# The eighth w1 row of each partition by five small loads of its own, and fewer small VectorE operations, in a one-core decode kernel

## The chip, the cores and the metric

The kernel runs on one core of one Trainium2 chip. The metric is device time in microseconds (us) of one execution; lower is better. Engines are named as in the profile: PE is TensorE's matmul, PEld its weight load, DVE is VectorE, ACT is ScalarE, POOL is GpSimd, SP is SyncE, whose queue issues nearly all loads here.

## What is computed

One token of a decoder: grouped-query attention over a key/value cache, and a small MLP block beside it, both on the same normalized input, summed with the input.

```python
x  = A_x; xn = layernorm(x)                      # 1 x 1024
out = x + A(xn, k_cache, v_cache, wq, wo) + B(xn, w1, w2, w3, w4)
# A: 32 query heads, 4 key/value heads, 65536 keys of 128
q = (xn @ wq);  p = softmax(q k^T / sqrt(128));  A = (p v) @ wo
# B: h = gelu(layernorm(xn) @ w1), quarters of h shifted by one or two tokens
x1 = xn + shifted(h) @ w2
B  = x1 + gelu(layernorm(x1) @ w3) @ w4          # w3: 1024 x 3584, w4: 3584 x 1024
```

With one token, each shift of the quarters brings in nothing but zeros, so h @ w2 adds zero; the kernel computes it all the same. All matrices and the cache are bfloat16: 169.87 MB are read from HBM once.

## The kernel before

The work is a list of items: wq, then for each key/value head g and each half r of its keys a K block and a V block (8.39 MB each), with w3, "wa" (w1 and the first half of w4), "wb" (the rest of w4, and w2) and wo between them. Three SBUF slots of 64 KB a partition take the items in turn. `load(i)` (L211) issues item i's DMAs on SP's queue once the readers of that slot are done; the main loop (L566) computes item i and then issues the load of item i + 3. In the order of the list: wq, K(0,0), V(0,0), w3, K(0,1), V(0,1), wa, K(1,0), V(1,0), K(1,1), and so on; wb stands before the last V, wo at the end, in five pieces (`WO_PIECES`).

Weights lie with one row block a partition: of w1 (1024 x 1024) partition p holds rows 8p to 8p + 7, so each partition reads 16 KB in one piece, and `rows_product` (L314) multiplies column c of the normalized input with row c of every partition, c from 0 to 7, in two chunks of 512 columns that lie in different column groups of TensorE (`tile_position`).

K blocks are transposed 32 by 32 on VectorE (L449, four of 4.4 us), multiplied with the queries (L455, 64 matmuls), reduced to a maximum (L462), turned into exponentials on ScalarE (L471), and transposed again (L473). V blocks are multiplied by these (L503). At the end of a head `group_weights` (L479) and `group_end` (L513) scale and fold the halves; the last lines (L524 to L529) put a head's result into oT as bfloat16. `compute_wa` (L405) multiplies by w1 (L408), applies gelu (L410), moves the row into columns (L419 to L425) and adds the first half of w4's product (L426, L337).

Order is kept by a small recorder, `Flow`: each operation names keys that it reads and writes, and waits on semaphores for the last writer and the readers of these. An engine's own order is the order in the code. A load's semaphore counts 16 when it is complete. The setup (L243 to L286) builds identity matrices on GpSimd and masks from them on VectorE, while the first loads are on their way.

Of the kernel before, what the change touches and what calls it, by code (L numbers as in the profile page):

```python
# [16 lines left out]
WO_PIECES = (10, 10, 8, 3, 1)  # L17
WO_UNROLL = 5
CGS = 2


class Flow:
# [75 lines left out]
def kernel(  # L98
# [43 lines left out]
    def tile_sb(shape, dtype, name):  # L142
        return sb.tile(shape, dtype, name=name)
# [27 lines left out]
    hf_f = tile_sb([P, FC], F32, "hf_f")  # L171
    hT = tile_sb([P, FC], BF16, "hT")
    gT = tile_sb([P, DC], BF16, "gT")
    o5 = tile_sb([P, 32], F32, "o5")
    oT = tile_sb([P, OC], BF16, "oT")
    rep = msk[0:1].rearrange("p a b -> p (a b)")

    sc = ps.tile([P, HF, 512], F32, name="sc")
# [6 lines left out]
    w3_v = B_w3.rearrange("(p c) f -> p (c f)", c=DC)  # L185
    w4_v = B_w4.rearrange("(m c) n -> m (c n)", c=FC)
    wo_v = A_wo.rearrange("(m c) n -> m (c n)", c=OC)
    w1_v = B_w1.rearrange("(p c) n -> p (c n)", c=DC)
    w2_v = B_w2.rearrange("(m c) n -> m (c n)", c=DC)
    assert sum(WO_PIECES) == OC  # L190
    wo_start = [sum(WO_PIECES[:i]) for i in range(len(WO_PIECES))]
# [19 lines left out]
    def load(i):  # L211
        item, s = items[i], slot_of[i]
        t, kind = slots[s], items[i][0]
        if kind == "wq":
            loads = [(0, wq_v)]
        elif kind == "w3":
            loads = [(0, w3_v)]
        elif kind == "wa":
            loads = [(0, w1_v), (KEYS // 2, w4_v[:, 0:FH * NOUT])]
        elif kind == "wb":  # L220
            loads = [(0, w4_v[:, FH * NOUT:FC * NOUT]), (KEYS // 2, w2_v)]
        elif kind == "wo":
            loads = [(wo_start[q] * NOUT, wo_v[:, wo_start[q] * NOUT:(wo_start[q] + n) * NOUT])
                     for q, n in enumerate(WO_PIECES)]
        else:
            cache = A_k_cache if kind == "K" else A_v_cache
            _, g, r = item
            loads = [(0, cache[0, g, r * KEYS:(r + 1) * KEYS, :].rearrange("(p k) d -> p (k d)", p=P))]
        fl._wait("Q", [], [("slot", s), ("slot", s, 1)] + [("slot", s, q) for q in range(2, 5)] + [("kt", s, cg) for cg in range(4)])
        for n, (at, src) in enumerate(loads):  # L230
            key = ("slot", s) if n == 0 else ("slot", s, n)
            fl.dma("Q", f"slot{s}" if n == 0 else f"slot{s}_{n}", [], [key], t[:, at:at + src.shape[-1]], src)

    qrow = work[:, 0:1024].rearrange("p (b n) -> p b n", b=2)
    psel = work[:, 1024:1536].rearrange("p (b m) -> p b m", b=4)
# [26 lines left out]
    def v(reads, writes, call):  # L262
        one("V", reads, writes, call)

    v(["ident_f"], ["sel32"], lambda e: e.tensor_tensor(out=sel32[:], in0=ident_f[:, 0:32], in1=ident_f[:, 32:64], op=ALU.add))
    v(["ident_f", "sel32"], ["sel32"], lambda e: e.tensor_tensor(out=sel32[:], in0=sel32[:], in1=ident_f[:, 64:96], op=ALU.add))
    v(["ident_f", "sel32"], ["sel32"], lambda e: e.tensor_tensor(out=sel32[:], in0=sel32[:], in1=ident_f[:, 96:128], op=ALU.add))
# [5 lines left out]
    v(["sel8"], ["sel8x"], lambda e: e.tensor_copy(out=sel8x[:].rearrange("p (h dd) -> p h dd", dd=4),  # L273
                                                   in_=sel8[:].unsqueeze(2).to_broadcast([P, 8, 4])))
    iv = ident_bf[:].rearrange("p (b i r) -> p b r i", b=2, r=2)
    for b in range(2):
        for par in range(2):
            v(["ident_bf"], [("psel", b, par)], lambda e: e.tensor_copy(
                out=psel[:, 2 * b + par, :].rearrange("p (a i) -> p a i", a=4),
                in_=iv[:, b, par, :].unsqueeze(1).to_broadcast([P, 4, 32])))  # L280
    psel_keys = [("psel", b, par) for b in range(2) for par in range(2)]
    lead = ident_bf[:].rearrange("p (j u) -> p j u", u=32)[:, :, 0]
    v(["ident_bf", "hstrip"], ["hstrip"], lambda e: e.tensor_copy(
        out=hstrip[:, 64:128].rearrange("p (j m) -> p j m", j=4), in_=lead.unsqueeze(2).to_broadcast([P, 4, 16])))
    v(["ident_bf"], ["gsel"], lambda e: e.tensor_copy(
        out=gsel[:].rearrange("p (j m) -> p j m", j=2), in_=lead[:, 0:2].unsqueeze(2).to_broadcast([P, 2, 64])))  # L286

    def layernorm(src, src_key, n):
# [22 lines left out]
    v([("rs", 0)], ["ln_s1"], lambda e: e.tensor_scalar(out=ln_s1, in0=rs1, scalar1=1.0, scalar2=None, op0=ALU.add))  # L311
    v([("neg", 0), ("rs", 0)], ["ln_s2"], lambda e: e.tensor_tensor(out=ln_s2, in0=neg1, in1=rs1, op=ALU.mult))

    def rows_product(s, keys, wt, width, n_chunks):  # L314
        def emit(signal):
            for c in range(DC):
                for j in range(4):
                    for bk in range(2):
                        ch = 4 * bk + j
                        if ch < n_chunks:  # L320
                            ins = nc.tensor.matmul(sc[32 * j:32 * j + 32, bk, 0:width], lhsT=xpad[:, c, :],  # L321
                                                   rhs=wt[:, c, ch * width:(ch + 1) * width],
                                                   start=(c == 0), stop=(c == DC - 1), tile_position=(0, 32 * j),
                                                   skip_group_check=True)
            signal(ins)
        op("T", keys + ["xpad"], ["sc"], emit)

# [15 lines left out]
    def fill_qst(g, eng):  # L343
        for a in range(4):
            sl = slice(32 * a, 32 * a + 32)
            one(eng, ["qsel"], [("qst", g % 2)],
                lambda e: e.tensor_copy(out=qst[g % 2][sl, :, 24 + 32 * a:24 + 32 * a + 8], in_=qsel[sl, :, 8 * g:8 * g + 8]))  # L347

    def compute_wq(s):
# [20 lines left out]
            signal(ins)  # L370
        op("T", ["qT"] + psel_keys, ["pm"], emit2)
        v(["pm"], ["qsel"], lambda e: e.tensor_copy(out=qsel[:], in_=pq))
        fill_qst(0, "V")
        fill_qst(1, "G")
        v(["xn2b", "xpad"], ["xpad"], lambda e: e.tensor_copy(out=xpad[:, :, 0:1], in_=xn2b[:].unsqueeze(2)))
        v(["xr", "ln_s1", "ln_s2"], ["ob"], lambda e: e.tensor_scalar(
# [9 lines left out]
    def compute_w3(s):  # L386
        wt = slots[s][:, 0:DC * F].rearrange("p (c n) -> p c n", n=F)
        rows_product(s, [("slot", s)], wt, FW, 8)
        hrow = work[:, 0:2 * FW].rearrange("p (b n) -> p b n", b=2)
        one("S", ["sc"], ["hrow", "work"], lambda e: e.activation(out=hrow, in_=sc[:, 0:2, 0:FW], func=ACTF.Gelu_apprx_tanh))  # L390

        def emit(signal):
            for bk in range(2):
                ins = nc.tensor.matmul(pm[:, 0:FW], lhsT=hstrip[:, 64 - 64 * bk:192 - 64 * bk], rhs=hrow[:, bk, :],  # L394
                                       start=(bk == 0), stop=(bk == 1))
            signal(ins)
        op("T", ["hrow", "hstrip"], ["pm"], emit)
        hm = work[:, 1024:1024 + 2 * FW].bitcast(F32).rearrange("p (a c) -> p a c", c=FC)
        v(["pm", "mask16"], ["hm"], lambda e: e.tensor_tensor(  # L399
            out=hm, in0=pm[:, 0:FW].rearrange("p (a c) -> p a c", c=FC),  # L400
            in1=mask16[:].unsqueeze(2).to_broadcast([P, 16, FC]), op=ALU.mult))
        v(["hm"], ["hf_f"], lambda e: e.reduce_sum(out=hf_f[:], in_=hm.rearrange("p a c -> p c a"), axis=AX.X))
        v(["hf_f"], ["hT"], lambda e: e.tensor_copy(out=hT[:], in_=hf_f[:]))

    def compute_wa(s):  # L405
        slot = slots[s]
        wt = slot[:, 0:DC * D].rearrange("p (c n) -> p c n", n=D)
# [5 lines left out]
        for grp, shift in enumerate((1, -1, 2, -2)):  # L413
# [10 lines left out]
        v(["gm"], ["gf"], lambda e: e.reduce_sum(out=lnb[:, 7], in_=gm.rearrange("p a c -> p c a"), axis=AX.X))  # L424
        v(["gf"], ["gT"], lambda e: e.tensor_copy(out=gT[:], in_=lnb[:, 7]))  # L425
# [53 lines left out]
    def group_weights():  # L479
# [33 lines left out]
    def group_end(g):  # L513
# [4 lines left out]
        if g == HKV - 1:  # L518
# [8 lines left out]
        v(["msk"], ["o5"], lambda e: e.tensor_reduce(out=o5[rows, :], in_=msk[rows].rearrange("p dd c -> p c dd"),  # L527
                                                     axis=AX.X, op=ALU.add))
        v(["o5"], ["oT"], lambda e: e.tensor_copy(out=oT[rows, :], in_=o5[rows, :]))  # L529

    fold = work[0:1, :].bitcast(F32)
    started = [False] * 4
# [73 lines left out]
```

## Time and profile before

| what | us |
|---|---|
| median of three runs (402.16 to 402.35) | 402.19 |
| the profiled execution | 402.23 |
| its span in the profile | 400.1 |
| PE busy | 223.5 (56%) |
| DVE busy | 210.5 (53%) |
| ACT busy | 30.9 (8%) |
| POOL busy | 6.3 (2%) |
| SP's main DMA queue (q1), share of 16 engines | 98.3% |
| DMA, mean over the span | 425 GB/s |

The profile is of one execution; what lies between its span and its own time, 2.1 us, is start and end of the execution. A line of a view by time gives the start, the busy time, the engine, the line of the code and the operation; in brackets, how long the engine sat idle before and what released it. A line of the queues gives the queue, its kind, packets, MB and its share of the 16 DMA engines in the window asked for; a packet counts in the window in which it starts, so shares of short windows can be above 100%. A line by stretch gives the window, its length, the busy time of each engine with its instructions, the granted TensorE clock, the DMA share and GB/s. The trace also has each DMA packet's start, duration and size, and the time of each of the completions (one per DMA engine that took part) by which a load counts its semaphore up.

### The profile page before, as it was taken

Reading aid. Unit: us, or ns where it says so; the run is one execution under the profiler, and the core shown is the slowest. Engines: PE = TensorE matmul, PEld = TensorE weight load, DVE = VectorE, ACT = ScalarE, POOL = GpSimd, SP = SyncE. Lnnn points to the kernel's source line nnn. Section 1 sums busy time; section 2 is a strip of 40 time slices with the busy share of each in tenths; the row PEclk is TensorE's granted clock in tenths of the full one; section 3 lists DMA queues with packets and bytes.
Section 4 is the critical chain, followed back from the end, with each engine's and each line's share of the span. In section 5 each row is a group of like instructions: output and inputs, shape, how many; then the busy total and the mean of one; then the engine's idle time right before and its main releaser. Section 6 shows DMA issues by size and latency. Waiting matters only on the chain.

```text
span 400.1 us, 4118 instructions
## 1 busy us (share of the span) xinstructions
PE 223.5 (56%) x1407; PEld 91.3 (23%) x1407; DVE 210.5 (53%) x191; ACT 30.9 (8%) x36; POOL 6.3 (2%) x28
## 2 busy tenths in 40 slices
PE   0263087360195563964395608845925194596985
PEld 0220033130042220421142203312402041232332
DVE  2201792210962448822972499269455963794421
ACT  1000000320001300003001000020020002000200
POOL 3000000000000000000000000000000000000000
PEclk9995579585589598795699567968988599799799
DMA  8999999999989999999999999999999999999995
GB/s 347 465 446 419 420 414 454 391 473 452 426 382 471 451 426 414 426 432 432 465 434 426 419 426 439 426 472 428 426 419 434 439 419 459 398 454 434 397 432 208
DMA packets 4054, 170.02 MB, mean 425 GB/s; under 512 B 582, under 2 KB 588, under 8 KB 844
## 3 DMA queue, kind: packets, MB, share of 16 engines
q1 hardware_dynamic: 3896, 169.87, 98.3%
q8 instruction: 8, 0.13, 0.1%
q10 hardware_dynamic: 148, 0.00, 0.0%
q14 instruction: 2, 0.02, 0.0%
HBM read 169.87 MB, written 0.00 MB: 425 GB/s over the span
## 4 chain that ended last, share of the span: by engine, by line
DMA 53%; PE 28%; DVE 13%; issue 4%; ACT 1%; SPq 1%; POOL 0%; ACTq 0%
DMA slot<-in_A_k_cache_dram 46%; PE sc L455 20%; DVE slot L449 10%; DMA slot<-in_A_wo_dram 7%; PE oacc L503 5%; PE psR L337 2%; DVE sm L462 2%; DVE work L473 1%; ACT work L471 1%; SPq L89 1%; PE sc L321 0%; DVE og L515 0%; ACT L471 0%; DVE sm L464 0%; PE pm L463 0%
## 5 line engine op out<-in xcount | busy, mean ns | idle before, releaser
L455 PE MATMUL sc<-slot,qst 128*128 x512 | 127.8, 407 | 77.4 <-DVE slot L449 76.4
L449 DVE STREAM_TRANSPOSE slot<-slot 128x4096 f32<-128x4096 f32 x32 | 139.4, 4413 | 29.7 <-DMA slot<-in_A_k_cache_dram 29.7
L455 PEld LDWEIGHTS sc<-slot,qst 128*128 128x128 bf16 x512 | 51.8, 101 | 154.2 <-issue 106.8
L503 PE MATMUL oacc<-slot,work 128*32 128x512 bf16 x512 | 45.7, 530 | 37.5 <-DVE work L473 21.9
L462 DVE TENSOR_REDUCE sm<-sc 128x1 f32<-128x2048 f32 x8 | 18.3, 2291 | 58.4 <-PE sc L455 58.4
L503 PEld LDWEIGHTS oacc<-slot,work 128*32 128x32 bf16 x512 | 19.0, 127 | 60.8 <-issue 56.9
L473 DVE STREAM_TRANSPOSE work<-work 128x2048 bf16<-128x2048 bf16 x8 | 18.5, 2312 | 21.2 <-ACT work L471 21.2
L471 ACT ACTIVATE work<-sc,sm 128x2048 bf16<-128x2048 f32 x8 | 15.7, 1967 | 147.1 <-DVE sm L469 147.1
L337 PE MATMUL psR<-slot,hT 128*1 x56 | 16.2, 438 | 0.5 <-issue 0.2
L515 DVE SCALAR_TENSOR_TENSOR og<-oacc,sm,og 128x128 f32<-128x128 f32 x16 | 5.6, 351 | 18.6 <-PE oacc L503 18.2
L321 PE MATMUL sc<-slot,xpad 128*32 128x512 bf16 (+1 forms) x144 | 11.1, 441 | 4.3 <-DMA slot<-in_A_wq_dram 4.3
L471 ACT ACT_TABLE_LOAD x3 | 3.8, 1283 | 117.5 <-DVE sm L469 117.5
L463 PE MATMUL pm<-ident_f,sm 128*1 128x128 f32 x8 | 2.2, 270 | 19.1 <-DVE sm L462 19.1
L294 PE MATMUL pm<-sm,og 128*128 128x1 f32 x4 | 1.2, 363 | 14.9 <-DVE sm L293 14.9
L337 PEld LDWEIGHTS psR<-slot,hT 128*1 x56 | 5.1, 92 | 10.9 <-issue 7.8
L321 PEld LDWEIGHTS sc<-slot,xpad 128*32 128x32 bf16 x144 | 5.4, 113 | 9.0 <-DMA slot<-in_A_wq_dram 4.4
L399 DVE TENSOR_TENSOR work<-pm,mask 128x448 f32<-128x448 f32 x1 | 0.6, 624 | 11.0 <-PE pm L394 11.0
L463 PEld LDWEIGHTS pm<-ident_f,sm 128*1 128x1 f32 x8 | 0.6, 79 | 23.0 <-DVE sm L462 23.0
L352 DVE CAST work<-sc 128x512 bf16<-128x512 f32 x1 | 0.7, 690 | 9.2 <-PE sc L321 9.2
L347 POOL COPY qst<-qsel 32x32 bf16<-32x32 bf16 x12 | 2.5, 206 | 189.0 <-PE sc L455 161.8
L337 PE MATMUL psR<-slot,oT 128*1 x20 | 4.5, 379 | 1.6 <-DVE oT L529 1.6
L509 ACT COPY ob<-oacc 128x512 f32<-128x512 f32 x4 | 2.3, 585 | 33.1 <-PE oacc L503 33.1
(99 smaller groups left out, 71.6 us busy)
## 6 DMA issues: line engine op xcount, KB each, us to landing
slot<-in_B_w_dram SPq DMA_DIRECT2D x1, 7168.0 KB, 50.8
slot<-in_B_w_dram SPq DMA_DIRECT2D x2, 3584.0 KB, 31.9
slot<-in_A_wo_dram SPq DMA_DIRECT2D x2, 2560.0 KB, 19.5
slot<-in_B_w_dram SPq DMA_DIRECT2D x2, 2048.0 KB, 30.1
slot<-in_A_wo_dram SPq DMA_DIRECT2D x1, 2048.0 KB, 26.7
slot<-in_A_wo_dram SPq DMA_DIRECT2D x1, 768.0 KB, 28.1
slot<-in_A_wo_dram SPq DMA_DIRECT2D x1, 256.0 KB, 28.4
slot<-in_A_k_cache_dram SPq DMA_DIRECT2D x8, 36.1
```

The lines of the kernel that those rows point to most:

```text
L89: self.engines[eng].dma_start(out=out, in_=in_).then_inc(sem, 16)
L321: ins = nc.tensor.matmul(sc[32 * j:32 * j + 32, bk, 0:width], lhsT=xpad[:, c, :], rhs=wt[:, c, ch * width:(ch + 1) * width], start=(c == 0 ...
L337: ins = nc.tensor.matmul(psR[0:1, h, :], lhsT=lv[:, bass.ds(c, 1), u], rhs=wv[:, bass.ds(c, 1), u, h, :], start=False, stop=False, skip_gr ...
L347: lambda e: e.tensor_copy(out=qst[g % 2][sl, :, 24 + 32 * a:24 + 32 * a + 8], in_=qsel[sl, :, 8 * g:8 * g + 8]))
L449: v([("slot", s)], [("kt", s, cg)], lambda e: e.transpose(out=kf[:, cg, :], in_=kf[:, cg, :]))
L455: ins = nc.tensor.matmul(sc[:, bass.ds(hf, 1), :], lhsT=qst[g % 2][:, bp, 24 - 8 * cg:24 - 8 * cg + P], rhs=kr[:, cg, bass.ds(hf, 1), :, b ...
L462: v(["sc"], ["mx"], lambda e: e.reduce_max(out=mx, in_=sc[:].rearrange("p h n -> p (h n)"), axis=AX.X))
L463: one("T", ["mx", "ident_f"], ["pm"], lambda e: e.transpose(pm[0:1, 0:P], mx, ident_f[:]))
L471: one("S", ["sc", ("nball", r)], WORK + [("lall", r)], lambda e: e.activation(out=pT, in_=sc[:], func=ACTF.Exp, bias=nball[:, r:r + 1], sc ...
L473: v(["work"], ["work"], lambda e: e.transpose(out=pT, in_=pT))
L503: ins = nc.tensor.matmul(oacc[32 * u:32 * (u + 1), :], lhsT=pT[:, hf, 32 * t:32 * (t + 1)], rhs=vt[:, :, hf, t, :], start=(hf == 0 and t < 4),
L515: v(["oacc", ("wm", 1), "og"], ["og"], lambda e: e.scalar_tensor_tensor(out=og[:, 0:P], in0=oacc[:, P * cg:P * (cg + 1)], scalar=wm[:, 1, ...
```

## The change

First, w1's load takes only seven of the eight rows of each partition (14 KB of each 16). The eighth rows of all 128 partitions come by five loads, issued between w1's and w4's: the first 100 of them by four loads of five partitions with five rows each (to partitions a, a + 4, ..., a + 16 for a = 0 to 3), and the last 28 by one load of 14 partitions with two rows each. They lie behind w1 in the same slot, row by row, so a partition now holds eighth rows of others; to match, seven small matmuls with columns of the identity gather the eighth column of the input into `xe`, two copies bring it to SBUF, and 14 matmuls with one column of weights take the place of the last two of `rows_product`. The five loads share one semaphore; all later loads wait for them.

Second, small VectorE operations go: ten of the setup and four that fill `qst` move to GpSimd; the casts behind four kinds of reductions go, since the reductions now write bfloat16; two multiplications of `wm` per head become one with broadcasts. That is 24 fewer in the program, and the two copies more.

```diff
+XP = 20
+XR = 5
+XQ = 14
...
-    w1_v = B_w1.rearrange("(p c) n -> p (c n)", c=DC)
+    w1_v = B_w1.rearrange("(p c) n -> p (c n)", c=DC)[:, 0:(DC - 1) * D]
+    w1_last = B_w1.rearrange("(p c) n -> p c n", c=DC)[:, DC - 1, :]
+    X_AT = DC * D
...
-        fl._wait("Q", [], [("slot", s), ("slot", s, 1)] + [("slot", s, q) for q in range(2, 5)] + [("kt", s, cg) for cg in range(4)])
+        fl._wait("Q", [], [("slot", s), ("slot", s, 1)] + [("slot", s, q) for q in range(2, 5)] + [("few", a) for a in range(5)] + [("kt", s, cg) for cg in range(4)])
...
+            if kind == "wa" and n == 0:
+                few = w1_last[0:XP * XR].rearrange("(i a r) n -> a i r n", a=4, r=XR)
+                for a in range(4):
+                    fl.dma("Q", "few", [], [("few", a)],
+                           t[a:a + XP - 3:4, X_AT:X_AT + XR * D].rearrange("p (r n) -> p r n", n=D), few[a])
+                fl.dma("Q", "few", [], [("few", 4)], t[0:XQ, X_AT + XR * D:X_AT + (XR + 2) * D].rearrange("p (r n) -> p r n", n=D),
+                       w1_last[XP * XR:P].rearrange("(p r) n -> p r n", r=2))
...
-    v(["ident_f"], ["sel32"], lambda e: e.tensor_tensor(out=sel32[:], in0=ident_f[:, 0:32], in1=ident_f[:, 32:64], op=ALU.add))
+    g_one(["ident_f"], ["sel32"], lambda e: e.tensor_tensor(out=sel32[:], in0=ident_f[:, 0:32], in1=ident_f[:, 32:64], op=ALU.add))
...
-        fill_qst(0, "V")
+        fill_qst(0, "G")
...
-    def rows_product(s, keys, wt, width, n_chunks):
+    def rows_product(s, keys, wt, width, n_chunks, n_c=DC, more=()):
         def emit(signal):
-            for c in range(DC):
+            for c in range(n_c):
...
+            for lhsT, c in more:
+                for j in range(n_chunks):
+                    ins = nc.tensor.matmul(sc[32 * j:32 * j + 1, 0, 0:width], lhsT=lhsT,
+                                           rhs=wt[0:lhsT.shape[0], c, j * width:(j + 1) * width],
+                                           start=False, stop=(c == DC + XR + 1), tile_position=(0, 32 * j),
+                                           skip_group_check=True)
...
-        v(["hm"], ["hf_f"], lambda e: e.reduce_sum(out=hf_f[:], in_=hm.rearrange("p a c -> p c a"), axis=AX.X))
-        v(["hf_f"], ["hT"], lambda e: e.tensor_copy(out=hT[:], in_=hf_f[:]))
+            v(["hm"], ["hT"], lambda e: e.reduce_sum(out=hT[:], in_=hm.rearrange("p a c -> p c a"), axis=AX.X))
...
-        rows_product(s, [("slot", s)], wt, 512, 2)
+        last = xn2b[:, DC - 1:DC]
+
+        def emit(signal):
+            for r in range(XR):
+                nc.tensor.matmul(pm[0:XP, r:r + 1], lhsT=ident_bf[:, r:XP * XR:XR], rhs=last, start=(r == 0), stop=False,
+                                 skip_group_check=True)
+            for r in range(2):
+                ins = nc.tensor.matmul(pm[0:XQ, XR + r:XR + r + 1], lhsT=ident_bf[:, XP * XR + r:P:2], rhs=last, start=False,
+                                       stop=(r == 1), skip_group_check=True)
+            signal(ins)
+        op("T", ["xn2b", "ident_bf"], ["pm"], emit)
+        v(["pm"], ["xe"], lambda e: e.tensor_copy(out=xe[0:XP, 0:XR], in_=pm[0:XP, 0:XR]))
+        v(["pm"], ["xe2"], lambda e: e.tensor_copy(out=xe[0:XQ, XR:XR + 2], in_=pm[0:XQ, XR:XR + 2]))
+        rows_product(s, [("slot", s), "xe", "xe2"] + [("few", a) for a in range(5)], wt, 512, 2, n_c=DC - 1,
+                     more=[(xe[0:XP if r < XR else XQ, r:r + 1], DC + r) for r in range(XR + 2)])
...
-        for r in range(NT):
-            v(["dmask", "wts"], [("wm", r)], lambda e: e.tensor_scalar(
-                out=wm[:, r, :], in0=dmask[:], scalar1=wts[:, r:r + 1], scalar2=None, op0=ALU.mult))
+        v(["dmask", "wts"], [("wm", r) for r in range(NT)], lambda e: e.tensor_tensor(
+            out=wm, in0=dmask[:].unsqueeze(1).to_broadcast([P, NT, 4]), in1=wts.unsqueeze(2).to_broadcast([P, NT, 4]), op=ALU.mult))
```

The gT and oT casts go in the same way as hT's, and the other moved lines of the setup (L266, L267, L273, L278, L283, L285) as the one shown.

More of the change, by code (lines that the diff above doesn't have):

```diff
@@ L170 @@
     qT = tile_sb([P, HQ], BF16, "qT")
-    hf_f = tile_sb([P, FC], F32, "hf_f")
     hT = tile_sb([P, FC], BF16, "hT")
     gT = tile_sb([P, DC], BF16, "gT")
-    o5 = tile_sb([P, 32], F32, "o5")
     oT = tile_sb([P, OC], BF16, "oT")
+    xe = tile_sb([P, 8], BF16, "xe")
     rep = msk[0:1].rearrange("p a b -> p (a b)")
@@ L187 @@
     wo_v = A_wo.rearrange("(m c) n -> m (c n)", c=OC)
-    w1_v = B_w1.rearrange("(p c) n -> p (c n)", c=DC)
+    w1_v = B_w1.rearrange("(p c) n -> p (c n)", c=DC)[:, 0:(DC - 1) * D]
+    w1_last = B_w1.rearrange("(p c) n -> p c n", c=DC)[:, DC - 1, :]
+    assert XP * XR + 2 * XQ == P
+    X_AT = DC * D
     w2_v = B_w2.rearrange("(m c) n -> m (c n)", c=DC)
@@ L263, in v, with g_one @@
         one("V", reads, writes, call)
-    v(["ident_f"], ["sel32"], lambda e: e.tensor_tensor(out=sel32[:], in0=ident_f[:, 0:32], in1=ident_f[:, 32:64], op=ALU.add))
-    v(["ident_f", "sel32"], ["sel32"], lambda e: e.tensor_tensor(out=sel32[:], in0=sel32[:], in1=ident_f[:, 64:96], op=ALU.add))
-    v(["ident_f", "sel32"], ["sel32"], lambda e: e.tensor_tensor(out=sel32[:], in0=sel32[:], in1=ident_f[:, 96:128], op=ALU.add))
+    def g_one(reads, writes, call):
+        one("G", reads, writes, call)
+    g_one(["ident_f"], ["sel32"], lambda e: e.tensor_tensor(out=sel32[:], in0=ident_f[:, 0:32], in1=ident_f[:, 32:64], op=ALU.add))
+    g_one(["ident_f", "sel32"], ["sel32"], lambda e: e.tensor_tensor(out=sel32[:], in0=sel32[:], in1=ident_f[:, 64:96], op=ALU.add))
+    g_one(["ident_f", "sel32"], ["sel32"], lambda e: e.tensor_tensor(out=sel32[:], in0=sel32[:], in1=ident_f[:, 96:128], op=ALU.add))
     v(["sel32"], ["mask16"], lambda e: e.tensor_tensor(out=mask16[:], in0=sel32[:, 0:16], in1=sel32[:, 16:32], op=ALU.add))
@@ L272 @@
     v(["sel32"], ["sel8"], lambda e: e.reduce_sum(out=sel8[:], in_=sel32[:].rearrange("p (cg h) -> p h cg", h=8), axis=AX.X))
-    v(["sel8"], ["sel8x"], lambda e: e.tensor_copy(out=sel8x[:].rearrange("p (h dd) -> p h dd", dd=4),
+    g_one(["sel8"], ["sel8x"], lambda e: e.tensor_copy(out=sel8x[:].rearrange("p (h dd) -> p h dd", dd=4),
                                                    in_=sel8[:].unsqueeze(2).to_broadcast([P, 8, 4])))
@@ L277 @@
         for par in range(2):
-            v(["ident_bf"], [("psel", b, par)], lambda e: e.tensor_copy(
+            one("G", ["ident_bf"], [("psel", b, par)], lambda e: e.tensor_copy(
                 out=psel[:, 2 * b + par, :].rearrange("p (a i) -> p a i", a=4),
@@ L282 @@
     lead = ident_bf[:].rearrange("p (j u) -> p j u", u=32)[:, :, 0]
-    v(["ident_bf", "hstrip"], ["hstrip"], lambda e: e.tensor_copy(
+    one("G", ["ident_bf", "hstrip"], ["hstrip"], lambda e: e.tensor_copy(
         out=hstrip[:, 64:128].rearrange("p (j m) -> p j m", j=4), in_=lead.unsqueeze(2).to_broadcast([P, 4, 16])))
-    v(["ident_bf"], ["gsel"], lambda e: e.tensor_copy(
+    one("G", ["ident_bf"], ["gsel"], lambda e: e.tensor_copy(
         out=gsel[:].rearrange("p (j m) -> p j m", j=2), in_=lead[:, 0:2].unsqueeze(2).to_broadcast([P, 2, 64])))
@@ L401, in compute_w3 @@
             in1=mask16[:].unsqueeze(2).to_broadcast([P, 16, FC]), op=ALU.mult))
-        v(["hm"], ["hf_f"], lambda e: e.reduce_sum(out=hf_f[:], in_=hm.rearrange("p a c -> p c a"), axis=AX.X))
-        v(["hf_f"], ["hT"], lambda e: e.tensor_copy(out=hT[:], in_=hf_f[:]))
+        with nc.allow_low_precision(reason="one term of the sum is not zero"):
+            v(["hm"], ["hT"], lambda e: e.reduce_sum(out=hT[:], in_=hm.rearrange("p a c -> p c a"), axis=AX.X))
     def compute_wa(s):
         slot = slots[s]
-        wt = slot[:, 0:DC * D].rearrange("p (c n) -> p c n", n=D)
-        rows_product(s, [("slot", s)], wt, 512, 2)
+        wt = slot[:, 0:X_AT + (XR + 2) * D].rearrange("p (c n) -> p c n", n=D)
+        last = xn2b[:, DC - 1:DC]
[12 more added lines that the diff above has]
+                     more=[(xe[0:XP if r < XR else XQ, r:r + 1], DC + r) for r in range(XR + 2)])
         h1row, grow = work[0:64, 0:512], work[0:64, 512:1024]
@@ L423, in compute_wa @@
             in1=mask64[:].unsqueeze(2).to_broadcast([P, 64, DC]), op=ALU.mult))
-        v(["gm"], ["gf"], lambda e: e.reduce_sum(out=lnb[:, 7], in_=gm.rearrange("p a c -> p c a"), axis=AX.X))
-        v(["gf"], ["gT"], lambda e: e.tensor_copy(out=gT[:], in_=lnb[:, 7]))
+        with nc.allow_low_precision(reason="one term of the sum is not zero"):
+            v(["gm"], ["gT"], lambda e: e.reduce_sum(out=gT[:], in_=gm.rearrange("p a c -> p c a"), axis=AX.X))
         rows_loop(hT[:, 0:FH], slot[:, KEYS // 2:KEYS // 2 + FH * NOUT], FH, ["hT", ("slot", s, 1)], unroll=2)
@@ L526, in group_end @@
             in1=mask4[rows, :].unsqueeze(2).to_broadcast([32, 4, 32]), op0=ALU.mult, op1=ALU.mult))
-        v(["msk"], ["o5"], lambda e: e.tensor_reduce(out=o5[rows, :], in_=msk[rows].rearrange("p dd c -> p c dd"),
-                                                     axis=AX.X, op=ALU.add))
-        v(["o5"], ["oT"], lambda e: e.tensor_copy(out=oT[rows, :], in_=o5[rows, :]))
+        with nc.allow_low_precision(reason="one of the four terms is not zero"):
+            v(["msk"], ["oT"], lambda e: e.tensor_reduce(out=oT[rows, :], in_=msk[rows].rearrange("p dd c -> p c dd"),
+                                                         axis=AX.X, op=ALU.add))
     fold = work[0:1, :].bitcast(F32)
```

## The prediction

> **What bounds the kernel now.** I read the page's slices and queues first, then three stretches of the span, then the chain of waits, then the queue that issues the loads.
>
> ```profile
> DMA  8999999999989999999999999999999999999995
> ...
> q1 hardware_dynamic: 3896, 169.87, 98.3%
> q8 instruction: 8, 0.13, 0.1%
> ```
>
> See that the DMA engines are busy all along, at 8 or 9 tenths up to the last slice (a packet is counted where it starts, so neighbouring slices swing), while TensorE has 56% and VectorE 53%. The same by stretch (the last two columns are DMA share and GB/s):
>
> ```profile
> 2.00:396.60 394.60, 223.21 (x1403) 91.20 (x1403) 210.04 (x190) 30.87 (x36) 5.29 (x22) 0.80 1.00 431
> 396.60:400.10 3.50, 0.28 (x4) 0.09 (x4) 0.42 (x1) 0.00 (x0) 0.00 (x0) 0.93 0.00 1
> ```
>
> From 2.0 to 396.6 us all 16 engines work without a gap that shows (share 1.00); 8.39 MB, one cache load, take 19.5 us at 431 GB/s. The end of the chain:
>
> ```profile
> 368.24 28.37 DMA slot<-in_A_wo_dram
> 396.60 0.04 issue
> 396.65 0.31 PE sc L536 x4
> 396.96 0.02 issue
> 396.98 0.42 DVE ob L560
> ```
>
> So the time is 2.0 us of start, the stream, and 3.5 us of fixed tail. An edit counts only if it changes the bytes or packets of the slowest engine, starves the queue, or touches that tail. Is the queue ever starved?
>
> ```profile
> 124.76 0.33 SPq L89 DMA_DIRECT2D slot<-in_A_k_cache_dram  x1
> 140.92 0.33 SPq L89 DMA_DIRECT2D slot<-in_A_v_cache_dram  x1
> 153.83 0.33 SPq L89 DMA_DIRECT2D slot<-in_A_k_cache_dram  x1
> ```
>
> K(1,0), issued at 124.76, is transposed from 151.11 (timeline); its 19.5 us of moving began at about 131.6. So it stood 6.9 us in the queue. V(1,0) then lands at about 170.6; the load issued at 153.83 stood 16.8 us. There is cover.
>
> **Why engines differ.** The trace records each DMA packet. One of 64 KB took 2.418 us, 28 KB 1.062, 20 KB 0.761, 16 KB 0.611, 6 KB 0.234, 2 KB 0.084: 9 ns and 36.7 ns a KiB or so. All engines get equal bytes. But the eight 16 KB packets of q8 (instructions) each hold up one of them:
>
> ```profile
> q1 hardware_dynamic: 9, 0.59, 107.1%
> q8 instruction: 1, 0.02, 4.4%
> ```
>
> This is the window 56 to 57.3 us; 4.4% of 16 x 1.3 us is 0.92 us. The 64 KB packet behind it took 2.924 instead of 2.418: 1.4 us in all. Followed packet by packet, the eight fall on eight different engines (at 56, 88, 152, 210, 272, 306, 363, 394.6), and two 8 KB ones of q14 (46.3 and 381.0, about 0.84 each) on a ninth. The sixteen completions of the last wo load agree: seven at 394.66 to 395.18, nine at 396.11 to 396.60. The kernel ends with its nine held-up engines; the others finish about 1.4 us sooner. Perfect balance would give the mean, (7 x 394.9 + 9 x 396.4)/16 = 395.7: at most 0.9 us to be had.
>
> **The change part by part.**
>
> *The eighth row.* Before, each engine moves eight 16 KB packets for w1, 4.89 us. After, eight of 14 KB (0.536 by the line above, 4.29) and the small loads. A load of five partitions should run on five engines: the trace shows a load of two rows (x, for the row form) as two data packets and two completions:
>
> ```profile
> DMA packets 36, 2.10 MB, mean 525 GB/s; under 512 B 2, under 2 KB 4, under 8 KB 4
> ...
> q10 hardware_dynamic: 4, 0.00, 0.2%
> ```
>
> The four then put 4 x 5 rows of 2 KB on the same five engines, the fifth two rows on each of 14. With 0.084 a row and 9 ns a completion: the five get 22 x 0.084 + 5 x 0.009 - 0.60 = +1.29 us; the next nine 2 x 0.084 + 0.009 - 0.60 = -0.42; the last two -0.60. If the five are engines that no fetch holds up, they go from about 394.8 to 396.1 (the latest of the early ones, 395.18, to 396.5), and the held-up ones from 396.60 to 396.18. The new end is about 396.2 to 396.3: **-0.35 us**.
>
> [...]
>
> *Price of five more loads.* On SP 0.33 to 0.43 us each, 2.2 us after 86.26; SP's next issue is at 124.76, so this is covered. On the engines, more packets can't be a gain; the one end is the wo tail: the last piece (256 KB, 2 KB packets) was used at 396.65, 0.72 us behind the one before at 395.93, and eight packets are 0.67. So no gap per load; I take only the 9 ns.
> The other end is that each small load costs its engines a whole round trip: the out store was issued at 397.43 and complete at 399.09, 1.66 us with nothing beside it; five in a row are 8.3 us (a rival, below). I take the wo tail, which is the nearer row: loads queued behind each other.
> [...]
>
> *The wait that is added.* Each later load waits for the small loads; first K(1,0). V(0,1) lands at about 131.6 - 13.4 = 118.2 (the 5.77 MB of the wa loads by 431 GB/s); then 4.29 + 1.9 gives 124.4, before SP is free at 124.76 anyway. If it came later, 6.9 us of queue stand behind it, and the other loads behind SP with it.
>
> *TensorE and VectorE in the w1 stage.* Two matmuls go, 14 and seven small ones come, and two copies.
>
> ```profile
> 142.69 1.89 PE L321 MATMUL sc<-slot,xpad 128*32 128x512 bf16 x15
> ```
>
> That is 0.12 us a matmul. The seven write pm, so they wait for VectorE's reading (L524, to 143.42), take 0.4 to 0.6 (L359: eight in 0.36), the copies 2 x 0.16 to 0.23 and hand-overs: rows start at about 144.6 instead of 142.69. 28 x 0.12 ends at 148.0 instead of 144.6: +3.4 us; at L337's 0.26 for the 14 one-column ones, +5.4. Below nothing it can't fall: nothing in front gets shorter. I take 3.4. Behind it on TensorE stand w4's rows, and the issue at 153.83 becomes 157 to 159: its 16.8 us of cover keep 11. VectorE's L421 and L424 slip to about 151.5, so K(1,0)'s transposes start 0.4 us late (2.2 at most), and with them the load at 176.30, which K(1,1), landing at 189.9, covers by 13 us. Without cover this part would cost 3 to 5 us.
>
> *The rest.* 24 VectorE operations go or move, about 0.17 to 0.37 us each (L265 0.19, L273 0.37, L278 0.25, L486 0.22, L529 0.17). None is on the path: ten are setup, done at 5.2 us, and VectorE then waits for x until 13.41. On GpSimd, at 0.2 to 0.6 us each, they end by 11 us at the latest (its memsets end at 4.4); the last that VectorE's order needs, sel32, at some 6. qst by GpSimd (1.04 for four) is needed at 51.49. The last group's cast is 0.17 us ahead of oT, after which TensorE waits for wo anyway. Zero, either side. Uncovered they'd give 4 us.
>
> *Instruction packets.* 38 to 40 more TensorE instructions at 143 us shift its fetches slightly earlier: the one at 394.6, which now holds up its engine by 0.93, may come at about 390 and cost 1.4; that engine is among the late. I take 0.0 to 0.3 of loss, and 0.05 in the sum.
> [...]
>
> **Sum.** 402.23 (the profiled execution; span 400.1 and 2.1 around it) - 0.40 + 0.05 = 401.88; the median of the runs, 402.19, is 0.04 lower: 401.85. A measurement here can tell about 0.2%, 0.8 us, from no change, so this is "the same".
>
> **The rivals.**
> *The five engines are held-up ones.* This is the one that ends slower. If one of the five is hit by a q8 packet, its end goes from at most 396.6 to 397.9: 403.1 to 403.5. It decides as soon as a single one of the five is among the eight. Against: the two engines of the two-row load (packets at 14.78 and 15.02) are among the seven early ones. For: in the first load, the engines' first packets start in an order that begins with those two; if it is the order of the engines, the fourth is q14's and the fifth is hit. 0.28.
> *One of the five is the ninth*, held up by q14. Those packets seem to come with VectorE's program (at 46.3 us it alone is at work), which is 22 instructions shorter; with one of the two left, the end is about 394.8 + 0.84 + 1.29 = 396.9: 402.0 to 402.7. With both, the case above. 0.18.
> *Each small load costs a round trip* on its five engines: 8.3 us less their 1.4 of lead and 0.6 for the row they lose, 408 to 409. It decides if a load's packets wait for the completion of the load ahead, which the wo tail doesn't show. 0.02. [...]
> *The loads don't spread over five engines* but go to one: 100 rows x 0.084 = 8.4 us less 0.6 and its 1.4 of lead: about 408. The two-row load speaks against. 0.02.
> *More is gained than the packets say* (fetches that vanish with the shorter program): to the bound, 401.3 and below. 0.05.
> *As forecast*, 401.5 to 402.0: 0.45.
>
> Faster by 0.2% (under 401.4): 0.04. Slower (over 403.0): 0.28 with part of the others, 0.33. The same: 0.63. The range reaches from 401.4 to 403.5.
>
> **What would show it.** Completions of the last wo load drawn together, within about 0.5 us, ending near 396.2: right. Five (or one) of them at 397.4 or later: the slower rival. q8 packets still eight, q14 in the span one or two. w1 packets of 14 KB, 100 + 28 packets of 2 KB. The load issued at 153.83 now 3 to 5 us later, with the DMA share still 1.00; TensorE's rows of w1 3 to 5 us longer. A slice with a DMA digit under 9 in the middle would overthrow the whole argument.

## The result, and the profile after

The changed kernel takes 403.21 us (median of 15 runs, 402.79 to 403.58) against 402.29 of the kernel before in the same runs (402.09 to 402.70): ratio 1.0021, 95% interval 1.0013 to 1.0029. It is slower by 0.9 us. Its profiled execution took 403.39, span 401.3. Medians below are of the executions in which the traffic ran at its full rate; the profiled execution of e9 was a slower one, so of e9 only the median is used.

The same lines of the page as before, with q14 added:

```profile
DMA  8999999999999999999999999999999999999994
...
q1 hardware_dynamic: 4058, 169.87, 98.2%
q8 instruction: 8, 0.13, 0.1%
...
q14 instruction: 1, 0.01, 0.0%
```

The same by stretch, before and behind the stage in which w1 and the first half of w4 are loaded:

```profile
2.00:116.70 114.70, 44.44 (x316) 19.30 (x316) 46.85 (x44) 8.52 (x10) 6.29 (x27) 0.76 1.00 431
131.00:395.00 264.00, 169.60 (x1028) 68.28 (x1028) 156.57 (x120) 19.23 (x25) 1.33 (x5) 0.81 1.00 432
```

The queue is never empty (DMA share 1.00); the bytes are the same; there are still eight q8 packets, and one q14 packet instead of two. The end of the chain, and the timeline's line for the last piece of wo (start, length, engine, work, idle before and its releaser):

```profile
395.20 0.04 issue
395.25 2.89 PE sc L570 x48
398.13 0.02 issue
398.16 0.42 DVE ob L594
```

```profile
397.71 0.09 PEld L570 LDWEIGHTS sc<-slot,oT 128*1 128x1 bf16 x4 [0.33 <-DMA slot<-in_A_wo_dram]
```

The last four matmuls start when the last piece has landed, at 397.7 instead of 396.6; the chain draws them together with the pieces before. From their start to the cast it is 0.45 us instead of 0.33. So 1.07 of the 1.16 us between the two profiled executions lie in the stream of loads. Its last sixteen completions, one for each DMA engine, are the key: three at 394.99 to 395.03, twelve at 396.22 to 396.94, and **one alone at 397.67**. Before, they ended together at 396.60.

Who is that one? When the loads of the w1 stage are complete, five engines are behind, as the change wants: nine completions at 130.39 to 130.67, two at 131.70 and 131.78 (by their lateness the two that q8 held up at 56 and 88 us), five at 132.06 to 132.52. Then come two instruction packets (window 141.3 to 143.5):

```profile
q1 hardware_dynamic: 15, 0.98, 106.2%
q8 instruction: 1, 0.02, 3.0%
q14 instruction: 1, 0.01, 0.9%
```

After them, at the landing of K(1,0), one of the nine has joined the late group, and one of the five stands alone at 152.47, 0.66 us behind the next. It stays alone to the end. The other q8 packets (195 to 392 us) each take one more of the early engines away, until three are left: as far as the completions show, q8 never hits one of the five.

The second thing is the stage itself. From the first completion of V(0,1) to that of w4's half it took 13.32 us before (116.62 to 129.94) and 13.67 now (116.72 to 130.39), for engines that should need 0.42 us less: they lost 0.77 us. The mean over all sixteen engines says the same: between these two loads it took 14.15 us instead of 13.35, and from there to the last completions 265.1 instead of 265.3. So the loss lies in this stage and nowhere behind it. The stage, after and before (the last two columns are DMA share and GB/s):

```profile
116.70:131.00 14.30, 7.89 (x36) 3.28 (x34) 2.94 (x4) 3.12 (x2) 0.81 (x4) 0.91 1.05 433
```

```profile
116.70:131.00 14.30, 8.46 (x39) 3.52 (x37) 2.94 (x4) 2.56 (x2) 0.81 (x4) 0.96 1.06 457
```

And 121 to 123.5 us in it, after and before:

```profile
121.00:123.50 2.50, 2.50 (x13) 1.05 (x11) 0.00 (x0) 0.00 (x0) 0.00 (x0) 1.00 1.11 415
```

```profile
121.00:123.50 2.50, 2.50 (x13) 1.14 (x12) 0.00 (x0) 0.00 (x0) 0.00 (x0) 1.00 1.12 483
```

The engines are as busy, with fewer bytes: packets take longer. The 14 KB packets took 0.578 us on the mean (0.536 forecast), the 28 KB packets behind the small loads 1.092 (1.063 before), 1.17 to 1.22 those that start before 123. With eight of each on an engine that is 0.34 and 0.23 us. The rest, 0.2 us, is not traced to packets: the 2 KB packets took 0.090 instead of 0.084, which is 0.01 us for two.

SP's queue:

```profile
86.02 5.09 SPq L92 DMA_DIRECT2D slot<-in_B_w_dram  x7
124.39 0.33 SPq L92 DMA_DIRECT2D slot<-in_A_k_cache_dram  x1
139.89 0.33 SPq L92 DMA_DIRECT2D slot<-in_A_v_cache_dram  x1
159.72 0.33 SPq L92 DMA_DIRECT2D slot<-in_A_k_cache_dram  x1
```

From V(1,0)'s issue to K(1,1)'s it is 19.8 us instead of 12.9, as TensorE's w1 stage is longer (and its granted clock 0.66 there, 1.00 before). It costs nothing: V(1,0)'s last engine is done at 171.8, so the queue still holds work when K(1,1) is issued at 159.7.

### The profile page after: what moved, and what is told of

It reads as the page before. It is cut to its first block, busy times and chain, and to the rows that moved or that the text cites. A ratio compares the mean times of both kernels' runs of the same rounds, so it can differ in the third digit from the quotient of the medians.

```text
span 401.3 us, 4155 instructions
## 1 busy us (share of the span) xinstructions
PE 224.8 (56%) x1426; PEld 92.1 (23%) x1426; DVE 206.8 (52%) x169; ACT 30.9 (8%) x36; POOL 9.4 (2%) x42
## 4 chain that ended last, share of the span: by engine, by line
DMA 51%; PE 30%; DVE 13%; issue 4%; ACT 1%; SPq 0%; POOL 0%; ACTq 0%
DMA slot<-in_A_k_cache_dram 45%; PE sc L490 20%; DVE slot L484 10%; DMA slot<-in_A_wo_dram 7%; PE oacc L537 4%; PE psR L358 2%; DVE sm L497 2%; PE sc L336 1%; PE sc L342 1%; PE sc L570 1%; DVE work L508 1%; ACT work L506 1%; DVE og L549 0%; ACT L506 0%; SPq L92 0%
## 5 line engine op out<-in xcount | busy, mean ns | idle before, releaser
L537 PE MATMUL oacc<-slot,work 128*32 128x512 bf16 x512 | 42.3, 500 | 37.5 <-DVE work L508 21.9
L570 PE MATMUL sc<-slot,oT 128*1 128x256 bf16 x88 | 4.6, 346 | 2.0 <-DMA slot<-in_A_wo_dram 2.0
```

The source lines that it names most:

```text
L537: ins = nc.tensor.matmul(oacc[32 * u:32 * (u + 1), :], lhsT=pT[:, hf, 32 * t:32 * (t + 1)], rhs=vt[:, :, hf, t, :], start=(hf == 0 and t < 4),
L570: ins = nc.tensor.matmul(psB[32 * j:32 * j + 1, 0:NQ], lhsT=lhsT, rhs=w_row[:, NQ * j:NQ * (j + 1)], start=(not started[j]), stop=False, t ...
```

## The experiments

Theory A: the last engine is one of the five that carry the small loads, held up by VectorE's q14 packet as well, on top of a stage in which all engines lost time. Rivals: B, TensorE's longer stage and the late issues; C, the VectorE and GpSimd edits; D, small loads on a part of the engines cost the stage whichever engines they are. In the names, "hole" is the eighth row, 2 KB of each 16 in HBM, that w1's load skips. The column "last" is the last completion of wo's last piece in the profile.

| kernel | last, us | median, us | ratio to before (interval) |
|---|---|---|---|
| before | 396.60 | 402.2 to 402.4 | |
| changed; again (e12) | 397.67; 397.43 | 403.21; 402.96 | 1.0021 (1.0013 to 1.0029); 1.0020 (1.0011 to 1.0029) |
| e1 rows only | 398.02 | 403.72 | 1.0035 (1.0021 to 1.0048) |
| e2 VectorE part only | 396.60 | 402.25 | 1.0000 (0.9991 to 1.0009) |
| e3 even eighth row | 396.79 | 402.36 | 1.0005 (0.9996 to 1.0014) |
| e4 no hole | 397.15 | 402.89 | 1.0016 (1.0007 to 1.0025) |
| e5 without the 14-load | 397.22 | 402.81 | 1.0016 (1.0007 to 1.0025) |
| e6 half of the rows | 396.61 | 402.42 | 1.0006 (0.9997 to 1.0015) |
| e7 eight engines | 397.12 | 402.83 | 1.0015 (1.0006 to 1.0024) |
| e8 eight engines, no hole | 396.97 | 402.62 | 1.0008 (0.9999 to 1.0017) |
| e9 14-load spread | - | 403.00 | 1.0019 (1.0008 to 1.0029) |
| e10 three engines | 396.90 | 402.49 | 1.0006 (0.9997 to 1.0015) |
| e11 three and even | 396.78 | 402.71 | 1.0017 (1.0006 to 1.0028) |
| e13 14-load spread, again | 397.23 | 402.95 | 1.0020 (1.0010 to 1.0030) |
| e14 eight partitions | 397.58 | 403.09 | 1.0019 (1.0010 to 1.0029) |
| e15 two loads of 64 | 397.29 | 403.25 | 1.0026 (1.0014 to 1.0038) |

### Each part alone: e1 and e2

e1 is the kernel before with the five loads and their products; e2 the changed kernel with w1 loaded whole and the old product.

> The first part of the change alone: the eighth w1 rows by five loads, all VectorE and GpSimd operations as in the kernel before. Theory A (five engines): the stream ends with one of the five DMA engines that carry the small loads, because it is also the one that VectorE's instruction packets (queue q14) hold up. With the longer VectorE program there are two such packets, as before (46 and 381 us), each some 0.84 us, so the end is 0.8 us later than in the changed kernel: about 404.0 us, ratio to before 1.004. Theory B (TensorE's longer w1 stage and the loads issued late): the same as the changed kernel, 403.2. Theory C (the VectorE and GpSimd edits cost the time): back to 402.3.

> The second part alone: fewer VectorE operations, w1 loaded whole as before. Theory A: 402.3, the kernel before, with one q14 packet in the span instead of two, and the completions of the last wo load still about 1.9 us apart, since the engines that q8's packets hold up end last either way. Theory B: 402.3. Theory C: 403.2.

e1's queues:

```profile
q14 instruction: 2, 0.02, 0.0%
```

Two q14 packets, at 46.5 and 381.1, as before. One completion stands alone again, at 398.02, now 1.2 us behind the next (396.85); in the last load that is complete before the second packet it stood 0.28 us behind the next (377.65 against 377.37), in the first one behind it 1.25 (384.68 against 383.43). So the packet at 381.1 moved that one engine by 0.9 to 1.0, and it was the last one already, after the packet at 46.5. The median is 403.72, less than the 404.0 expected: the stage lost less here (14 KB packets 0.550). e2 takes as long as the kernel before (402.25). C falls, and the shorter VectorE program even helps, by the one packet, where the five loads are there.

### The five engines: e6 and e10

```diff
-                for a in range(4):
+                for a in range(2):                                   # e6
...
-                           t[a:a + XP - 3:4, X_AT:...], few[a])
+                           t[a:a + 9:4, X_AT:...], few[a][0:3])      # e10
```

> As the changed kernel, but two of the four loads of five partitions are left out (50 of the eighth rows are not loaded; the products run on what lies there, so TensorE's work is the same). The five engines have ten 2 KB packets less, 0.84 us. Theory A: the last completion comes down by that until the engines that q8 holds up are the last: from 397.67 to about 396.8 or 396.9, 402.4 to 402.6 us. Theory B: 403.2, as nothing on TensorE changes.

> As the changed kernel, but each of the four loads takes three partitions instead of five (40 of the eighth rows are not loaded; TensorE's work is the same), so that three engines carry 20 rows each. If the engine that VectorE's q14 packets hold up is among these three: 403.2, one completion 0.7 us behind all others as before. If it is the fourth or fifth: that last completion is gone, the end is that of the engines that q8 holds up, 396.8 or so, 402.4 to 402.6. In the first load of the kernel before, the first packets' starts would make it the fourth. Theory B: 403.2.

e10's chain (the last piece is used as it lands):

```profile
396.90 0.04 issue
396.95 0.31 PE sc L570 x4
```

Both take the lone completion away, with TensorE's work unchanged: 402.42 and 402.49, as A expected, where B expected 403.2. The engine that q14 holds up is one that a load of five partitions uses and a load of three does not. In e6 the stage is still slow (28 KB packets 1.085), in e10 too (1.096); the end is now that of the engines that q8 holds up.

### Where the stage loses: e3, e4, e5, e9, e13, e14, e15

```diff
+                fl.dma("Q", "few", [], [("few", 0)], t[:, (DC - 1) * D:DC * D], w1_last)      # e3: in place of the five
...
+    w1_v = B_w1[0:(DC - 1) * P].rearrange("(p c) n -> p (c n)", c=DC - 1)                     # e4
+    w1_last = B_w1[(DC - 1) * P:D]
...
-                       t[0:XQ, X_AT + XR * D:...
+                       t[0:9 * XQ:9, X_AT + XR * D:...                                        # e9, e13
+                       t[0:29:4, X_AT + XR * D:...  (three rows each)                         # e14
...
+                for a in range(2):                                                             # e15: e3's load in two
+                    fl.dma("Q", "few", [], [("few", a)], t[64 * a:64 * a + 64, (DC - 1) * D:DC * D], w1_last[64 * a:64 * a + 64])
```

e5 leaves the load of 14 out.

> As the changed kernel, but the eighth rows come by one load of 128 partitions with one row each, to their old place, and the product is the old one: the load is split, but even over all engines. By the packets' own durations this is +0.08 us over before. Theory A in its second half (in the w1 stage of the changed kernel all engines lost about 0.7 us; 14 KB packets took 0.578 instead of 0.536, because w1 is read with a hole of 2 KB in every 16): the hole is here too, so 402.6 to 403.0. If the lengthening comes from the five loads on few engines instead: 402.4. Theory B: 402.3, since TensorE's stage is the old one.

> As the changed kernel, with the same seven loads in size and engines, but w1's main load reads its first 896 rows, seven for each partition, in one piece without holes, and the small loads read the last 128 rows, one behind another. Rows of w1 so meet other elements of the input than in the reference; the work is the same. Theory A: 14 KB packets go back to 0.536, the stage is about 0.4 to 0.7 us shorter, and the five engines still end last: 402.5 to 402.8. If the hole is not the cause, and for theory B: 403.2.

> As the changed kernel, but the load of 14 partitions is left out (28 of the eighth rows are not loaded; the products run on what lies there). All engines have two rows less, 0.18 us, except the last two. Theory A: the order of the engines stays, so about 0.2 us less than the changed kernel, 403.0. If that load, which 14 engines write into 14 neighbouring partitions, is what makes the 28 KB packets behind it slow (1.09 instead of 1.06 us on the mean, in the kernels with the small loads but not in the one with an even load), these go back to 1.062 and another 0.2 us goes: 402.8. Theory B (TensorE's stage): 403.2.

> As the changed kernel, but the load of 14 partitions goes to partitions 0, 9, ..., 117 instead of 0 to 13 (the products read the old places, so part of them runs on what lies there). If the 28 KB packets are slowed because 14 engines write into neighbouring partitions, they go back to 1.062 us on the mean, and the time to about 403.0; if any load of 14 engines does it, they stay at 1.08 to 1.09, and the time at 403.2.

> The load of 14 partitions spread over 0, 9, ..., 117, a second time, since the first profile was of an execution in which all traffic was slower. If neighbouring partitions are what slows the 28 KB packets: 1.062 us, about 403.0. If engines that write to other partitions than those they write in a load of 128 partitions: still 1.08 to 1.10, 403.2.

> As the changed kernel, but in place of the load of 14 partitions one of eight (0, 4, ..., 28) with three rows each (four of the eighth rows are not loaded; the products read the old places). [...] If writing elsewhere is what slows the 28 KB packets, they are back at 1.062, the early completions of the stage come 0.2 us sooner, and the end is 397.67 + 0.08 - 0.2 = 397.5: 403.0. If not: 403.3.

> The even split again, by two loads of 64 partitions with one row each instead of one of 128. [...] If that is what slows the packets behind: 28 KB packets over 1.07 on the mean, 402.5 to 402.6. If only uneven loads do it: 1.062, 402.36 as in the even split.

Mean packet durations in the w1 stage, us:

| kernel | 14 KB | 28 KB behind |
|---|---|---|
| changed; e12; e1; e6; e10 (load of 14 to partitions 0 to 13) | 0.578; 0.580; 0.550; 0.564; 0.584 | 1.092; 1.086; 1.086; 1.085; 1.096 |
| e4 (the same loads, no hole) | 0.538 | 1.084 |
| e5 (no load of 14); e13 (spread); e14 (0, 4, ..., 28) | 0.570; 0.570; 0.554 | 1.063; 1.062; 1.062 |
| e3 (one load of 128); e7 (eight partitions, 0, 4, ... and 1, 5, ...) | 0.548; 0.553 | 1.062; 1.062 |
| e11 (load of 80); e15 (two loads of 64) | 0.547; 0.552 | 1.103; 1.142 |

Two losses show in the packets. The first follows the **destination**: 28 KB packets that start before about 124 us are slow in the kernels with a load to a closed run of partitions that covers a part of the 128 (0 to 13, 0 to 79, or 64 at a time), and back to the 1.062 of before when the load of 14 writes the same bytes to partitions 0, 9, ..., 117 (e13). e15 shows it best, with even bytes and nothing else changed from e3. 121 to 124 us of e3, e13 and e15:

```profile
121.00:124.00 3.00, 3.00 (x15) 1.24 (x13) 0.00 (x0) 0.00 (x0) 0.00 (x0) 1.00 1.23 521
```

```profile
121.00:124.00 3.00, 3.00 (x15) 1.34 (x14) 0.00 (x0) 0.00 (x0) 0.00 (x0) 1.00 1.11 467
```

```profile
121.00:124.00 3.00, 3.00 (x16) 1.29 (x14) 0.00 (x0) 0.00 (x0) 0.00 (x0) 1.00 1.11 362
```

Splitting one load of 256 KB into two of 64 partitions costs 0.9 us (403.25 against 402.36, where 402.5 to 402.6 was expected). Why the packets behind a closed run are slow no trace shows. That they are fits the 28 KB packets of e13 and e14 (spread, 1.062 both) and of e15 (1.142), but not those of e8 (below; spread, 1.084).

My stricter reading, that an engine must write the partitions it writes in a load of 128, gave 1.08 to 1.10 for the 28 KB packets of e13, and they took 1.062. That e13 tests it, and e14 and e15 with it, was my assumption: no trace shows which partitions an engine writes.

The second loss goes with the **source**: with w1 read without its hole the 14 KB packets take 0.538 (e4, and 0.539 in e8), in all the others 0.547 to 0.584, which is 0.1 to 0.4 us for eight. In e4 the small loads are read in larger packets too (10 and 4 KB). But of the 14 KB packets those that end before the first small packet starts already differ: 0.535 in e4, against 0.576 and 0.572 in the two profiles of the changed kernel, 0.542 in e1 and 0.544 in e3. Alone the hole costs no time that can be seen: e3 has it, was expected at 402.6 to 403.0 for that, and took 402.36. Why the packets of the same load vary so much between kernels, but little between two profiles of one kernel (0.578 and 0.580), I can't explain; that the hole takes part is shown, its mechanism is open.

How much is each worth? Counted as above, by the first completions and against the packets' own durations, the stage lost 0.77 and 0.75 us in the two profiles of the changed kernel, 0.55 in e1, 0.34 without the hole (e4), 0.31 with the load of 14 spread (e13), nothing in e3 and 1.0 in e15. So either remedy takes about 0.4 us off the stage in its profile. In the medians it does not stand out: 402.89 for e4 (402.5 to 402.8 expected), 402.95 and 403.00 for the load spread, against 403.21 and 402.96 for the changed kernel.

e14 has neither the load of 14 nor a gain: the five engines have a row more than in the changed kernel, and the profiled stream was already 0.26 us late before the stage (V(0,1) complete from 116.98); its median, 403.09, lies between the two expectations.

### Other shares: e7, e8, e11, e12

> The eighth rows by two loads of eight partitions with eight rows each, so on eight engines, 16 rows each: +0.77 us for the eight and -0.60 for the other eight, if q8's packets fall on the other eight. Theory A: the engine with one q14 packet ends at 394.8 + 0.3 + 0.85 + 0.77 = 396.7, those that q8 holds up at 396.0: 402.1 to 402.4 with little lost in the stage. Theory D (small loads on a part of the engines cost the whole stage 0.4 to 0.7 us, whichever engines): 402.6 to 403.0. If q8's packets fall on some of the eight: 403.3 or more, the last completion at 397.3 or later.

> As the one with eight engines, with w1's first 896 rows read in one piece, seven to a partition, and the last 128 for the small loads (rows of w1 meet other elements of the input; the work is the same). Packets of the small loads should be 16 KB instead of 2 KB, 0.61 instead of 8 x 0.084: +0.64 for the eight. Theory A: 402.0 to 402.2. Theory D: 402.5 to 402.9.

> All eighth rows again, in another share: 48 by four loads of three partitions with four rows, 80 by one load of 80 partitions with one row, on all 16 engines. Three engines carry 21 rows, +1.2 us; the others five, -0.17 us. Theory A, with the q14 engine not among the three: the end is that of the engines held up by q8, 396.6 - 0.17 + 0.1 for the hole = 396.5: 402.1 to 402.3, no difference that can be measured. With it among the three: 402.9 or more. If a load on part of the engines slows the stage again: 402.5.

> The changed kernel once more, on the same chip as these: 403.2. Its second profile tells how far the 14 KB packets of the w1 stage (0.578 us on the mean in its first profile, 0.550 with the same loads in the run of the first part alone) differ from one execution to the next: theory A takes 0.55 to 0.58 for the same thing, and the one late completion stays at 397.4 to 397.8.

In e7 three completions stand last, at 396.65, 397.06 and 397.12, where the other thirteen end by 395.94. I read them as the q14 engine and two that q8 hit later. Then two of the three engines that a load of eight uses beyond the five are q8's, and the forecast that its packets fall on the other eight was wrong. e8 is the same with 396.78 to 396.97. Its 28 KB packets take 1.084 although no load goes to neighbours; they are slow up to 126 us and again at 129, where those of the other kernels are back at 1.06, and that stays open. e11 ends with eleven engines together (396.55 to 396.78 in a profiled execution of 402.47), balanced as meant, and its median is still 0.5 us above before, where 402.1 to 402.3 was expected and D gave 402.5. Its 28 KB packets took 1.103: the load of 80 neighbouring partitions seems to cost the stage more than the balance gives. D is not ruled out: e7 and e8 also came out in the ranges that it gave. No kernel beats the one before by more than the interval; e2 and e3 equal it.

## Why the prediction was wrong

It gave 401.85, with a range from 401.4 to 403.5; 403.21 is in that range, but on the other side of no change: the forecast had a chance of 0.45 and "slower" 0.33. That 403.21 also falls within the price of the first rival, 403.1 to 403.5, is luck: that rival has a q8 packet on one of the five, and none fell there.

- **The failed step** is the condition "If the five are engines that no fetch holds up". It holds for q8 and fails for q14: one of the five is the ninth engine (e1, e6, e10). The rival with that name had it, even to "with one of the two left". Its end was put at 396.9, and without the next point it should have been that; the 0.77 us make it 397.7.
- **The second failed step** is the price of the moved row by "the line above", and "I take only the 9 ns". Durations of packets in loads of 128 partitions were carried over to a load with holes and to loads on a few neighbouring partitions, and there the 14 KB packets took 0.578 and the 28 KB packets behind 1.092. The mis-sized term is 0 to 0.05 us where 0.77 was measured. The row for the tail of wo that was used for it is of loads of 128 partitions.
- **Two terms that no trace of before shows.** That the four loads of five use the same five engines held: at the end of the stage five completions stand behind the others, at 132.06 to 132.52. The 0.05 for a q8 packet that comes earlier with more TensorE instructions was an estimate: after, five of the last six start earlier (142.3, 195.4, 260.5, 306.5, 349.9 and 391.6 instead of 151.9, 209.7, 272.2, 306.0, 363.2 and 394.6), and the last one took 0.94 us instead of 0.93; the last completion of all, at 397.67, was that of another engine.
- **Right**: the stream bounds the kernel, and nothing on TensorE, VectorE or SP reaches the time (e2 equals before; DMA share 1.00 in the profile after). The load of five partitions runs on five engines (the five small loads have 34 completions, 4 x 5 + 14), and the loads of three in e10 leave out the one that q14 holds up (last completion 396.90 instead of 397.67); each of the five gained 1.7 us of work against the others (130.5 to 132.3), as 1.29 + 0.42 says. Eight q8 packets as before.
- **Wrong at no cost**: the small loads take SP 0.86 us each on the mean (5.09 less 0.80 for the other two, over five), not 0.33 to 0.43; the w1 stage moves K(1,1)'s issue by 6.9 us against V(1,0)'s, not 3.4 to 5.4. The cover held.
- **The order of first packets** in the first load, used as weak evidence that the fourth engine is q14's, was borne out as far as e10 goes; for the fifth, which it made one of q8's, it was wrong.
- **Two slips in the working** matter little. The rows give 9 ns and 37.6 ns a KiB (from 2.418 for 64 KB and 0.084 for 2 KB), not 36.7; the 0.536 for 14 KB goes by the former and was met without the hole (0.535). And the end at 396.2 to 396.3 is worth 0.35 us against 396.60, where the sum takes 0.40.

## What to carry to other kernels

Where loads bound a kernel without a gap, look at the completions of one load engine by engine: what can be gained by balance is their maximum less their mean, here at most 0.9 us, and each engine that is to get more must first be known to have nothing else, instruction packets included. A small load can be paid for by the packets behind it: here 28 KB packets took 1.09 us behind the load of 14 on neighbouring partitions and 1.062 with it spread (e13), which the time does not show; in e8, spread too, they took 1.084. One load of 128 partitions in two halves cost 0.9 us here (e15). A cost taken from one shape of load need not hold for another: 14 KB packets were put at 0.536 by loads without a hole and took 0.578.

## What the hardware showed that was not expected

- Two loads of 64 partitions in place of one of 128, 256 KB in all, cost 0.9 us and lengthened 28 KB packets behind them from 1.062 to 1.142 us on the mean, and to as much as 1.53.
- The instruction packets of 8 KB (q14) went with VectorE's program: two in the span before and in e1, one in the changed kernel and in e2, where the program is shorter. In e1 both fell on one DMA engine: the one that was last already, by 0.28 us, was last by 1.25 behind the packet at 381 us. The eight of 16 KB (q8) fell on eight different ones. As read from the completions, none of them is one of the five that carry a load of five partitions, and two of them are among the three more that the loads of eight (e7) use.
- Issuing each of the five small loads took SP 0.71 to 0.96 us, against 0.33 to 0.44 for a load of 128 partitions (e3). The number of engines is not what sets it: the two loads of 64 in e15, each with sixteen completions, took 0.55 and 1.23.
- The TensorE clock granted in the changed w1 stage was 0.66, against 1.00 before; at the tail it was 0.50 (395 to 397.7 us), against 1.00 before (394.7 to 396.6). The 0.1 us more from the last matmuls' start to the cast goes with that.
